# First batch's softmax division at the attention outputs, and the first MoE's weight clamp on GpSimd

## The chip, the cores and the metric

The kernel runs on one core of one Trainium2 chip. The metric is the device time of one execution in microseconds (us). Three runs of the kernel before gave 967.96, 968.99 and 969.51 us, a median of 968.99 us. The engines are TensorE (PE for matmuls, PEld for weight loads), VectorE (DVE), ScalarE (ACT), GpSimd (POOL) and SyncE (SP), which issues the DMAs. Each of them works through its own instructions in order, and waits on semaphores that the others raise.

## The reference, cut to what matters

Three layers follow one another. Attention with a decay comes first (4 batches, 8 heads, 576 positions, 64 wide), then a mixture layer that takes the largest of three products, then a layer with a rational activation.

```python
scores = (q @ k.T) / sqrt(D) + cum[:, None] - cum[None, :]    # causal, cum = cumsum(log(clip(f)))
attn = exp(scores - max(scores))
attn = attn / (sum(attn, axis=-1) + 1e-09)                    # the division of the change
x  = attn @ v                                                 # 2304 tokens x 512
x  = max(x @ w1, x @ w2, x @ w3) @ w_out                      # first MoE, 512 -> 768 -> 512
h  = x @ w_in                                                 # second MoE, 512 -> 2048
g  = (a0 + a1*h + a2*h**2 + a3*h**3) / (1 + |b0|*|h| + |b1|*h**2 + 1e-6)
out = g @ w_out2                                              # 2048 -> 512
```

The weights of both MoE layers arrive in a 64-bit format, read as pairs of 32-bit integers (a low and a top half), and the kernel converts them itself.

## The kernel before, in words

Attention works on pairs of heads. The first batch is cut in two query groups (group 0: the first 320 positions in blocks of 64, 128 and 128; group 1: the last 256 in two blocks), so that it gives eight pairs, numbered 0 to 7: four with group 0, then four with group 1. The other batches give twelve pairs with both groups. A unit is one head of a pair in one group. The main loop takes one unit a step, in three stages that overlap: `scores` of unit s, `turn` of unit s-1, `attend` of the pair when both its heads are turned.

- `scores` (L324) multiplies queries and keys on TensorE. VectorE adds the mask and takes the row maximum (L347, then a read of the accumulator). ScalarE takes the exponential and leaves the row sum in the tile `rs` (L353).
- `normalise` (L355) adds 1e-9 to the row sums (L358) and takes the reciprocal (L359) on VectorE, and GpSimd multiplies every block of exponentials `e` with it in place (L362): three instructions a unit in group 0 (64, 192 and 320 columns), two in group 1 (448 and 576).
- `turn` transposes the blocks on TensorE (L382) into the PSUM tile `tp`, and ScalarE copies them to `pt` (L384).
- `attend` multiplies with v (L398), ScalarE rounds the result to the high part of `x` (L405), and VectorE subtracts to get the low part (L406). Of these two parts every later product is made, in three matmuls.

While the first pairs are worked on, the weights of the first MoE are converted in `convert` (L162), 18 pieces of 128x512 (`cv_w`) and 12 of 128x256 (`cv_wo`): ScalarE takes the absolute value (L169), VectorE clamps it (L170), masks and shifts (L171), and joins the halves in two steps (L172, L175), ScalarE makes the rounded high part (L178), GpSimd the low part (L179). The raw pieces lie in rings of buffers that come free with L175. `fill`, called six times a step, hands out these conversions (0.15 of one a call in the first seven steps, 0.5 later), and from step 9 on the first MoE of the batch that is done: 18 products `h` (L430 to L432), whose maximum is taken on VectorE (L437), then the four output products `x2p` (L455 to L457). In the early pairs (0 to 3), `exercised` adds two matmuls of 512 columns on a tile of identities, `warm`, to every bank that TensorE opens (L84).

The tile framework puts the instructions of each engine into an order that it works out from a model of their durations; the program's order gives the priorities. So a change of one instruction can move many others. Only the second MoE from its seventeenth step on stands in an order written by hand.

## Time and profile before

| | |
|---|---|
| median of three runs | 968.99 us |
| profiled execution | 970.9 us, span 969.1 us |
| mean granted TensorE clock | 0.988 |
| busy: PE, PEld | 943.1 us (97%), 829.9 us (86%) |
| busy: DVE, ACT, POOL | 739.6 us (76%), 623.8 us (64%), 252.4 us (26%) |

The busy time of TensorE counts matmuls that overlap, so it says where the engine stands still more surely than how fast it works. The lines of the change run in the first 160 us, so the rows are read by stage: 11 to 52 us is attention of group 0, 52 to 140 us is attention of group 1 with the first MoE and most of the conversions, 148 to 500 us are the other three batches.

### The profile page before, as it was taken

The page shows a single profiled execution, that of the slowest core. Times are in us where ns is not written, and L with a number is a line of the kernel's source. Part 1 is how long each engine was busy: PE and PEld are TensorE (multiplying, and loading weights), DVE is VectorE, ACT ScalarE, POOL GpSimd, SP SyncE. Part 2 cuts the span into 40 slices and gives each one's busy share as a digit, 9 for nine tenths or more (in the row PEclk, how much of TensorE's full clock was granted, in tenths as well). Part 3 has the DMA queues.
Part 4 walks back from the last instruction along what each step waited for, and adds up shares of the span by engine and source line. Part 5 has one row for each costly group of instructions (what it writes and reads, how often), then busy time and mean ns, then how long its engine had stood idle before and what let it go on. Part 6 is the DMA issues. An engine that isn't in the chain of part 4 may idle for free.

```text
span 969.1 us, 16846 instructions
## 1 busy us (share of the span) xinstructions
PE 943.1 (97%) x5780; PEld 829.9 (86%) x5780; DVE 739.6 (76%) x1756; ACT 623.8 (64%) x1457; POOL 252.4 (26%) x408
## 2 busy tenths in 40 slices
PE   7998999999999999999999999999999999999998
PEld 6767889998998988999999978888888888999997
DVE  5789985557777777534397949988888988899997
ACT  5875666667667666646454548767666766677775
POOL 2646553445454545425133400000000000000000
PEclk9978999999999999999999999999999999999999
DMA  6685233124446445230145477011002101100000
GB/s 160 159 236 153 64 83 89 43 63 119 140 131 205 133 136 174 58 94 1 57 140 185 132 253 269 1 44 43 1 1 66 44 1 46 64 1 1 34 1 33
DMA packets 125621, 88.52 MB, mean 91 GB/s; under 512 B 74448, under 2 KB 110304, under 8 KB 125536
## 3 DMA queue, kind: packets, MB, share of 16 engines
q1 hardware_dynamic: 125536, 87.45, 30.4%
q8 instruction: 46, 0.75, 0.4%
q14 instruction: 39, 0.32, 0.1%
HBM read 64.73 MB, written 22.69 MB: 90 GB/s over the span
## 4 chain that ended last, share of the span: by engine, by line
PE 70%; DVE 14%; DMA 6%; ACT 4%; issue 3%; POOL 2%; SPq 1%; ACTq 0%; POOLq 0%; DVEq 0%
PE oo L721 7%; PE oo L722 7%; PE oo L720 7%; PE hq L671 6%; PE hq L673 6%; PE hq L672 6%; PE tp L382 4%; PE h L430 4%; PE o L398 4%; PE h L431 4%; PE h L432 4%; PE x2p L455 2%; DMA raw_wi<-in_moe_w_in_dram 2%; PE x2p L456 2%; PE x2p L457 2%
## 5 line engine op out<-in xcount | busy, mean ns | idle before, releaser
L430 PE MATMUL h<-x,w1h 128*128 128x320 f32 (+1 forms) x576 | 176.6, 307 | 3.1 <-ACT m L435 2.2
L431 PE MATMUL h<-x,w1h 128*128 128x320 f32 (+1 forms) x576 | 172.1, 299 | 0.0
L432 PE MATMUL h<-x,w1l 128*128 128x320 f32 (+1 forms) x576 | 171.2, 298 | 0.0
L430 PEld LDWEIGHTS h<-x,w1h 128*128 128x128 f32 x576 | 109.4, 190 | 7.0 <-ACT m L435 3.0
L362 POOL TENSOR_SCALAR e<-e,rs 128x64 f32<-128x64 f32 (+4 forms) x160 | 87.7, 563 | 106.4 <-DVE rs L359 91.5
L353 ACT ACTIVATE e<-e,st 128x64 f32<-128x64 f32 (+4 forms) x160 | 89.1, 557 | 37.8 <-DVE st L347 36.0
L721 PE MATMUL oo<-wp,gh 128*128 128x512 f32 x288 | 112.9, 392 | 0.0
L720 PE MATMUL oo<-wp,gh 128*128 128x512 f32 x288 | 112.5, 390 | 0.0
L431 PEld LDWEIGHTS h<-x,w1h 128*128 128x128 f32 x576 | 109.5, 190 | 0.4 <-issue 0.2
L432 PEld LDWEIGHTS h<-x,w1l 128*128 128x128 f32 x576 | 109.2, 190 | 0.0
L722 PE MATMUL oo<-wp,gl 128*128 128x512 f32 x288 | 108.8, 392 | 0.0
L680 ACT ACTIVATE s<-hq 128x512 f32<-128x512 f32 (+1 forms) x80 | 44.3, 554 | 97.4 <-PE hq L673 97.4
L347 DVE CUSTOM_DVE_ANT_0 e<-s,mask 128x320 f32<-128x320 f32 (+3 forms) x160 | 67.2, 433 | 37.9 <-PE s L346 24.0
L384 ACT ACTIVATE pt<-tp 128x384 f32<-128x384 f32 (+3 forms) x160 | 69.8, 469 | 19.2 <-PE tp L382 17.4
L683 DVE SCALAR_TENSOR_TENSOR s<-s,ab,u 128x512 f32<-128x512 f32 (+1 forms) x80 | 55.7, 697 | 32.1 <-ACT u L681 31.9
L382 PE MATMUL tp<-ident,e 128*128 128x128 f32 (+1 forms) x480 | 78.0, 280 | 1.3 <-DVE k2s L275 0.6
L673 PE MATMUL hq<-x,wil 128*128 128x512 f32 (+1 forms) x192 | 70.4, 367 | 0.0
L671 PE MATMUL hq<-x,wih 128*128 128x512 f32 (+1 forms) x192 | 70.4, 367 | 0.0
L672 PE MATMUL hq<-x,wih 128*128 128x512 f32 (+1 forms) x192 | 70.3, 366 | 0.0
L722 PEld LDWEIGHTS oo<-wp,gl 128*128 128x128 f32 x288 | 54.1, 188 | 11.7
L720 PEld LDWEIGHTS oo<-wp,gh 128*128 128x128 f32 x288 | 54.2, 188 | 11.0
L721 PEld LDWEIGHTS oo<-wp,gh 128*128 128x128 f32 x288 | 54.1, 188 | 10.9
(129 smaller groups left out, 2433.6 us busy)
## 6 DMA issues: line engine op xcount, KB each, us to landing
raw_w<-in_moe_w_dram SPq DMA_DIRECT2D x18, 512.0 KB
raw_wp<-in_moe_w_out_dram SPq DMA_DIRECT2D x32, 256.0 KB
wpd<-wp SPq DMA_DIRECT2D x32, 256.0 KB
raw_wi<-in_moe_w_in_dram SPq DMA_DIRECT2D x32, 256.0 KB
wp<-wpd SPq DMA_DIRECT2D x10, 768.0 KB
x2d<-xo SPq DMA_DIRECT2D x16, 320.0 KB
out_dram<-ob SPq DMA_DIRECT2D x18, 256.0 KB
kn<-in_k_dram SPq DMA_DIRECT2D x32, 128.0 KB
```

The source lines that it names most:

```text
L353: nc.scalar.activation(e[:nr], e[:nr], AF.Exp, bias=m, scale=-1.0, accum_out=l)
L362: nc.gpsimd.tensor_scalar(e, e, self.rs[:, 1, j : j + 1], 0.0, op0=ALU.mult, op1=ALU.add)
L382: nc.tensor.transpose(tp[:kr, dst : dst + P], self.e[i][:, Q0[c] : Q1[c]], ident)
L430: nc.tensor.matmul(hp_[:, :w], wh[:, j, dc], xs[dc][:, 1], start=(dc == NDC - 1), stop=False)
L431: nc.tensor.matmul(hp_[:, :w], wh[:, j, dc], xs[dc][:, 0], start=False, stop=False)
L432: nc.tensor.matmul(hp_[:, :w], wl[:, j, dc], xs[dc][:, 0], start=False, stop=(dc == 0))
L671: nc.tensor.matmul(hp_[:, :w], wih[:, dc, fs], xh, start=(dc == 0), stop=False)
L672: nc.tensor.matmul(hp_[:, :w], wih[:, dc, fs], xl, start=False, stop=False)
L673: nc.tensor.matmul(hp_[:, :w], wil[:, dc, fs], xh, start=False, stop=(dc == NDC - 1))
L720: nc.tensor.matmul(o, g[0][:, ts_], wh_, start=(fc == 0), stop=False)
L721: nc.tensor.matmul(o, g[0][:, ts_], wl_, start=False, stop=False)
L722: nc.tensor.matmul(o, g[1][:, ts_], wh_, start=False, stop=(fc == NF2 - 1))
```

## The change: what it does

For the eight pairs of the first batch (`LATE`), `normalise` no longer touches the exponentials. The row sums of the two heads lie in one tile. When the second head is done, VectorE adds 1e-9 and takes the reciprocal for both at once (L369, L370 after), and GpSimd spreads the result over 64 columns a head into a tile `rx` (L374). In `turn`, TensorE transposes `rx`, one matmul a block, into a PSUM tile `rb` from the ring that the other transposes use (L407), and ScalarE copies it to a tile `rn` in SBUF (L411). In `attend`, VectorE multiplies the output with `rn` (L435), ScalarE rounds the product (L436) and VectorE subtracts (L437). Apart from that, the clamp of `convert` goes from VectorE to GpSimd (L171) for the 30 pieces of the first MoE; the pieces named `wp` and `wi`, of the second MoE, keep it on VectorE.

```diff
--- before.py
+++ after.py
@@ -113,6 +113,7 @@
 
 
     LOOK, WHOLE, PRE = 2, 6, 2
+    LATE = NPAIR * 2
     CONV2, EARLY = (32, 0.25), 12
     kqs = {}
 
@@ -167,7 +168,7 @@
         t = pool.tile(shape, I32, name=f"cv_{nm_}", tag=tag, bufs=bufs)
         tf = t.bitcast(F32)
         nc.scalar.activation(tf, top.bitcast(F32), AF.Abs)
-        nc.vector.tensor_scalar(tf, tf, E_LO, E_HI, op0=ALU.max, op1=ALU.min)
+        (nc.gpsimd if nm_[:2] != "wi" and nm_[:2] != "wp" else nc.vector).tensor_scalar(tf, tf, E_LO, E_HI, op0=ALU.max, op1=ALU.min)
         nc.vector.tensor_scalar(t, t, 0x07FFFFFF, 3, op0=ALU.bitwise_and, op1=ALU.logical_shift_left)
         nc.vector.scalar_tensor_tensor(
             out=t, in0=low, scalar=29, in1=t, op0=ALU.logical_shift_right, op1=ALU.bitwise_or
@@ -249,6 +250,7 @@
             self.iq = [[(2 * n + h) % m for h in range(2)] for m in NQB]
             self.pt = {}
             self.whole = n < WHOLE
+            self.late = n < LATE
             self.iqf = [(2 * n + h) % 4 for h in range(2)]
 
         def load(self):
@@ -319,7 +321,13 @@
 
         def begin(self):
             self.st = apool.tile([P, 9], F32, name=f"st_{self.nm}", tag="st", bufs=3)
-            self.rs = apool.tile([P, 2, 3], F32, name=f"rs_{self.nm}", tag="rs", bufs=3)
+            p = self.pair
+            if not p.late:
+                self.rs = apool.tile([P, 2, 3], F32, name=f"rs_{self.nm}", tag="rs", bufs=3)
+                return
+            if self.h == 0:
+                p.rs = apool.tile([P, 2, 2, 3], F32, name=f"rs_{self.nm}", tag="rsd", bufs=2)
+            self.rs = p.rs[:, :, self.h]
 
         def scores(self, i):
             p, h, g = self.pair, self.h, self.g
@@ -355,6 +363,16 @@
         def normalise(self):
             blks = GBLK[self.g]
             n = len(blks)
+            if self.pair.late:
+                if self.h == 1:
+                    rs = self.pair.rs
+                    nc.vector.tensor_scalar_add(rs[:, 0, :, :n], rs[:, 0, :, :n], 1.0e-9)
+                    nc.vector.reciprocal(rs[:, 1, :, :n], rs[:, 0, :, :n])
+                    rx = apool.tile([P, n, 2, D], F32, name=f"rx_{self.nm}", tag=("e3_", "e2_")[self.g] + str(self.pair.hp % 2))
+                    self.pair.rx = rx
+                    r = rs[:, 1, :, :n].rearrange("p h j -> p j h").unsqueeze(3).to_broadcast([P, n, 2, D])
+                    nc.gpsimd.tensor_scalar(rx, r, 1.0, 0.0, op0=ALU.mult, op1=ALU.add)
+                return
             nc.vector.tensor_scalar_add(self.rs[:, 0, :n], self.rs[:, 0, :n], 1.0e-9)
             nc.vector.reciprocal(self.rs[:, 1, :n], self.rs[:, 0, :n])
             for j, i in enumerate(blks):
@@ -382,6 +400,15 @@
                     nc.tensor.transpose(tp[:kr, dst : dst + P], self.e[i][:, Q0[c] : Q1[c]], ident)
                 n += hi - q0
             nc.scalar.activation(pt[:kr, base : base + n], tp[:kr, :n], AF.Copy)
+            if p.late and self.h == 1 and bank == len(GBANK[g]) - 1:
+                lo, w = GQ[g][0], GQ[g][1] - GQ[g][0]
+                rb = ps_t.tile([P, 512], F32, name=f"rb_{self.nm}", tag="t")
+                for j, i in enumerate(GBLK[g]):
+                    nc.tensor.transpose(
+                        rb[:, Q0[i] - lo : Q0[i] - lo + P], p.rx[:, j].rearrange("p h d -> p (h d)"), ident
+                    )
+                p.rb = mpool.tile([P, 320], F32, name=f"rn_{self.nm}", tag="mx", bufs=3)
+                nc.scalar.activation(p.rb[:, :w], rb[:, :w], AF.Copy)
 
         def attend(self):
 
@@ -402,6 +429,13 @@
                         if (j, i) != (0, 1):
                             pinned(mm)
             x = mpool.tile([P, 2, w], F32R, name=f"x_{self.nm}", tag=f"x{g}", bufs=(6, 8)[g])
+            xt[p.b, p.hp, g] = x
+            if p.late:
+                xn = p.rb
+                nc.vector.tensor_tensor(xn[:, :w], ot[:, :w], xn[:, :w], op=ALU.mult)
+                nc.scalar.activation(x[:, 0], xn[:, :w], AF.Copy)
+                nc.vector.tensor_tensor(x[:, 1], xn[:, :w], r32(x[:, 0]), op=ALU.subtract)
+                return
             nc.scalar.activation(x[:, 0], ot[:, :w], AF.Copy)
             nc.vector.tensor_tensor(x[:, 1], ot[:, :w], r32(x[:, 0]), op=ALU.subtract)
             xt[p.b, p.hp, g] = x
```

Three places show what this moves. The first is GpSimd's queue where the pieces of `w_out` are converted (`cv_wo`, then `wo` for the low part; `hh` is the low part of the first MoE's middle layer, `e` an exponential block). This is the kernel before:

```order
L179 TENSOR_TENSOR wo_1065<-cv_wo_0_1066,wo_1065 128x256
L362 TENSOR_SCALAR e_6_1_1_1357<-e_6_1_1_1357,rs_1_1_1356 128x448
L362 TENSOR_SCALAR e_6_1_1_1373<-e_6_1_1_1373,rs_1_1_1356 128x576
L179 TENSOR_TENSOR wo_1065<-cv_wo_1_1117,wo_1065 128x256
L179 TENSOR_TENSOR wo_1165<-cv_wo_0_1166,wo_1165 128x256
L443 TENSOR_TENSOR hh_0_3_1688<-m_0_0_3_1686,hh_0_3_1688 128x320
L179 TENSOR_TENSOR wo_1165<-cv_wo_1_1197,wo_1165 128x256
```

The same pieces in GpSimd's queue after the change:

```order
L171 TENSOR_SCALAR cv_wo_0_1063<-cv_wo_0_1063 128x256
L180 TENSOR_TENSOR w1l_948<-cv_w_5_1016,w1h_947 128x512
L171 TENSOR_SCALAR cv_wo_1_1113<-cv_wo_1_1113 128x256
L180 TENSOR_TENSOR wo_1062<-cv_wo_0_1063,wo_1062 128x256
L171 TENSOR_SCALAR cv_wo_0_1162<-cv_wo_0_1162 128x256
L180 TENSOR_TENSOR wo_1062<-cv_wo_1_1113,wo_1062 128x256
L171 TENSOR_SCALAR cv_wo_1_1193<-cv_wo_1_1193 128x256
L477 TENSOR_TENSOR hh_0_2_1479<-m_0_0_2_1477,hh_0_2_1479 128x320
L180 TENSOR_TENSOR wo_1161<-cv_wo_0_1162,wo_1161 128x256
L180 TENSOR_TENSOR wo_1161<-cv_wo_1_1193,wo_1161 128x256
L171 TENSOR_SCALAR cv_wo_0_1244<-cv_wo_0_1244 128x256
L171 TENSOR_SCALAR cv_wo_1_1264<-cv_wo_1_1264 128x256
```

The two multiplications of `e` are gone from between the subtractions, and each clamp stands behind one or two subtractions of earlier pieces.

The second is VectorE at the same pieces (`m` is a maximum of the first MoE), here in the kernel before:

```order
L170 TENSOR_SCALAR cv_wo_0_1166<-cv_wo_0_1166 128x256
L437 TENSOR_TENSOR m_0_0_3_1615<-m_0_0_3_1546,h_0_0_3_1602 128x320
L171 TENSOR_SCALAR cv_wo_0_1166<-cv_wo_0_1166 128x256
L172 SCALAR_TENSOR_TENSOR cv_wo_0_1166<-raw_wo_0_1063,cv_wo_0_1166 128x256
L175 SCALAR_TENSOR_TENSOR cv_wo_0_1166<-raw_wo_0_1063,cv_wo_0_1166 128x256
L170 TENSOR_SCALAR cv_wo_1_1197<-cv_wo_1_1197 128x256
L171 TENSOR_SCALAR cv_wo_1_1197<-cv_wo_1_1197 128x256
L437 TENSOR_TENSOR m_0_0_3_1686<-m_0_0_3_1615,h_0_0_3_1673 128x320
L172 SCALAR_TENSOR_TENSOR cv_wo_1_1197<-raw_wo_1_1115,cv_wo_1_1197 128x256
L175 SCALAR_TENSOR_TENSOR cv_wo_1_1197<-raw_wo_1_1115,cv_wo_1_1197 128x256
```

VectorE at these pieces after the change:

```order
L172 TENSOR_SCALAR cv_wo_0_1063<-cv_wo_0_1063 128x256
L173 SCALAR_TENSOR_TENSOR cv_wo_0_1063<-raw_wo_0_996,cv_wo_0_1063 128x256
L176 SCALAR_TENSOR_TENSOR cv_wo_0_1063<-raw_wo_0_996,cv_wo_0_1063 128x256
L435 TENSOR_TENSOR rn_1_1_1462<-o_1_1_1517,rn_1_1_1462 128x256
L172 TENSOR_SCALAR cv_wo_1_1113<-cv_wo_1_1113 128x256
L173 SCALAR_TENSOR_TENSOR cv_wo_1_1113<-raw_wo_1_1014,cv_wo_1_1113 128x256
L176 SCALAR_TENSOR_TENSOR cv_wo_1_1113<-raw_wo_1_1014,cv_wo_1_1113 128x256
L437 TENSOR_TENSOR x_1_1_1283<-rn_1_1_1213,x_1_1_1283 128x256
L172 TENSOR_SCALAR cv_wo_0_1162<-cv_wo_0_1162 128x256
L471 TENSOR_TENSOR m_0_0_2_1477<-m_0_0_2_1393,h_0_0_2_1464 128x320
L173 SCALAR_TENSOR_TENSOR cv_wo_0_1162<-raw_wo_0_1060,cv_wo_0_1162 128x256
L176 SCALAR_TENSOR_TENSOR cv_wo_0_1162<-raw_wo_0_1060,cv_wo_0_1162 128x256
```

A piece has three instructions in place of four, the first of which waits for GpSimd's clamp, and the multiplications `rn` and subtractions `x` of the attention outputs stand among them.

The third is TensorE where pair 8, the first of the second batch, begins (`s_0_8_0` and the like are its scores, `h_0_0_4` the fifth of six column blocks of the first MoE, `rb` the transposed reciprocals, `o` an attention output), here in the kernel before:

```order
L455 MATMUL x2p_0_0_2046<-hh_0_5_2004,wo_1488 128x320
L455 MATMUL x2p_0_1_2099<-hh_0_5_2004,wo_1488 128x320
L456 MATMUL x2p_0_0_2046<-hh_0_5_2004,wo_1488 128x320
L457 MATMUL x2p_0_0_2046<-hh_0_5_2004,wo_1488 128x320
L456 MATMUL x2p_0_1_2099<-hh_0_5_2004,wo_1488 128x320
L457 MATMUL x2p_0_1_2099<-hh_0_5_2004,wo_1488 128x320
L345 MATMUL s_0_8_0_0_1694<-k1s_1087,q1s_1621 128x64
L345 MATMUL s_0_8_0_0_1700<-k1s_1087,q1s_1621 128x192
L297 MATMUL tq_1_1633<-ident,qn_1429 128x128 x2
```

TensorE at the first scores of pair 8's second head after the change:

```order
L400 MATMUL tp_7_1_1_1667<-ident,e_7_1_1_1590 64x128
L354 MATMUL s_0_8_1_0_1762<-k2s_1090,q2s_1626 128x64
L353 MATMUL s_0_8_1_0_1768<-k1s_1089,q1s_1625 128x192
L354 MATMUL s_0_8_1_0_1768<-k2s_1090,q2s_1626 128x192
L407 MATMUL rb_1_1_1671<-ident,rx_1_1_1642 128x128 x2
L353 MATMUL s_0_8_1_0_1774<-k1s_1089,q1s_1625 128x320
L354 MATMUL s_0_8_1_0_1774<-k2s_1090,q2s_1626 128x320
L353 MATMUL s_0_8_0_1_1851<-k1s_1084,q1s_1153 128x448
L354 MATMUL s_0_8_0_1_1851<-k2s_1085,q2s_1154 128x448
L425 MATMUL o_1_1_1719<-pt_124,v_1422 64x256 x8
L425 MATMUL o_1_1_1719<-pt_124,v_1422 64x128 x2
L464 MATMUL h_0_0_4_1779<-x_1_0_836,w1h_848 128x320
```

Before, all 18 products `h` and half of `x2p` stand ahead of pair 8's scores. After, the scores stand ahead of the last five products `h` and of all of `x2p`. The transposes of `rx` are new.

## Rows read from the trace of the kernel before

**Rows 1.** Stages: us, busy us of PE, PEld, DVE, ACT, POOL (x instructions), PEclk, DMA share, GB/s.

```profile
11.00:52.00 41.00, 40.05 (x231) 31.25 (x232) 25.02 (x91) 31.59 (x94) 19.02 (x29) 1.00 0.65 171
52.00:62.00 10.00, 9.06 (x50) 5.87 (x48) 9.88 (x27) 8.87 (x23) 2.15 (x4) 1.00 1.13 318
62.00:80.00 18.00, 16.23 (x57) 10.43 (x57) 16.71 (x37) 10.93 (x26) 12.58 (x13) 0.53 0.61 166
80.00:124.00 44.00, 39.38 (x272) 36.19 (x271) 41.21 (x87) 25.92 (x64) 26.69 (x32) 1.00 0.39 112
124.00:140.00 16.00, 14.34 (x104) 12.61 (x102) 14.28 (x45) 12.06 (x33) 8.74 (x12) 1.00 0.18 46
140.00:148.00 8.00, 7.25 (x28) 6.72 (x29) 4.51 (x13) 3.71 (x11) 4.63 (x10) 0.57 0.54 152
148.00:500.00 352.00, 348.13 (x2733) 323.18 (x2732) 218.31 (x738) 221.85 (x637) 154.54 (x276) 1.00 0.37 104
...
570.00:969.00 399.00, 394.71 (x1801) 333.23 (x1799) 349.69 (x569) 275.01 (x490) 0.00 (x0) 1.00 0.14 49
```

**Rows 2.** Chain of waits, 50 to 150 us: start us, us, what.

```profile
58.42 1.47 DVE cv_w L175
...
61.74 0.74 POOL e L362
...
66.30 3.78 PE s L343 x6
```

**Rows 3.** VectorE groups, 52 to 140 us: busy us, mean ns, idle before, releaser.

```profile
L175 DVE SCALAR_TENSOR_TENSOR cv_w<-raw_w,cv_w 128x512 int32<-128x512 int32 x12 | 11.4, 953 | 0.1
...
L175 DVE SCALAR_TENSOR_TENSOR cv_wo<-raw_wo,cv_wo 128x256 int32<-128x256 int32 x12 | 7.0, 586 | 0.2
L170 DVE TENSOR_SCALAR cv_w<-cv_w 128x512 f32<-128x512 f32 x12 | 6.6, 550 | 1.2 <-ACT cv_w L169 1.1
...
L170 DVE TENSOR_SCALAR cv_wo<-cv_wo 128x256 f32<-128x256 f32 x12 | 5.3, 448 | 0.8 <-ACT cv_wo L169 0.8
...
L358 DVE TENSOR_SCALAR rs<-rs 128x2 f32<-128x2 f32 x8 | 3.0, 379 | 0.1
...
L359 DVE RECIPROCAL rs<-rs 128x2 f32<-128x2 f32 x8 | 1.3, 156 | 0.1
L406 DVE TENSOR_TENSOR x<-o,x 128x256 fp32r<-128x256 f32 x3 | 1.2, 416 | 0.5 <-ACT x L405 0.5
```

**Rows 4.** GpSimd busy on L362 alone, 0 to 145 us (x instructions).

```profile
0.00:145.00 145.00, 24.48 (x40) 0.93 0.53 142
```

**Rows 5.** GpSimd groups, 0 to 145 us.

```profile
L179 POOL TENSOR_TENSOR w1l<-cv_w,w1h 128x512 fp32r<-128x512 f32 x18 | 25.3, 1409 | 26.4 <-ACT w1h L178 26.2
L179 POOL TENSOR_TENSOR wo<-cv_wo,wo 128x256 fp32r<-128x256 f32 x12 | 8.8, 741 | 4.1 <-ACT wo L178 4.0
L362 POOL TENSOR_SCALAR e<-e,rs 128x576 f32<-128x576 f32 x8 | 7.2, 898 | 0.0
...
L362 POOL TENSOR_SCALAR e<-e,rs 128x448 f32<-128x448 f32 x8 | 5.7, 709 | 9.2 <-DVE rs L359 9.2
L362 POOL TENSOR_SCALAR e<-e,rs 128x320 f32<-128x320 f32 x8 | 4.7, 586 | 0.0
L362 POOL TENSOR_SCALAR e<-e,rs 128x192 f32<-128x192 f32 x8 | 4.3, 532 | 0.0
```

**Rows 6.** Chain of waits, three TensorE pieces of 10 to 150 us.

```profile
47.82 0.33 PE tp L382 x3
...
143.81 0.27 PE x2p L456
...
148.33 0.14 PE x2p L456
```

**Rows 7.** VectorE line L170, 0 to 160 us: duration ns min/median/max.

```profile
L170 DVE TENSOR_SCALAR cv_w<-cv_w x18: 400/422/1032, 21.6 to 99.7; 128x512 f32<-128x512 f32 x18
```

**Rows 8.** The page's costliest groups: the copy of the transposed weights of attention.

```profile
L384 ACT ACTIVATE pt<-tp 128x384 f32<-128x384 f32 (+3 forms) x160 | 69.8, 469 | 19.2 <-PE tp L382 17.4
```

## Prediction

> **What bounds the kernel now.** I read the table of stages first, then the chain of waits in the stages of the change, then the groups of VectorE and GpSimd there.
>
> The stages fall into three kinds [rows 1]. From 11 to 52 us TensorE is busy 40.05 of 41 us at full clock, much of it with the `warm` matmuls; VectorE is busy 25.0 us of it. From 52 to 140 us VectorE is the fullest: 9.88 + 16.71 + 41.21 + 14.28 = 82.1 of 88 us, or 93%, while TensorE stands still for 10 + 18 + 44 + 16 - (9.06 + 16.23 + 39.38 + 14.34) = 9.0 us, and in 62 to 80 us it has a granted clock of 0.53, the lower of its two levels (1.2 GHz). GpSimd is busy 50.2 of these 88 us. From 148 us on TensorE is busy 348.1 of 352 us, and at the end 394.7 of 399. So time won before 148 us reaches the end unless TensorE itself has to repay it, and nothing in the change shortens what comes behind.
>
> The chain of waits says the same of the middle stage: a join of 1.47 us on VectorE, then a GpSimd multiplication of `e`, then six score matmuls that take 3.78 us at the low clock [rows 2]. VectorE's queue delays the masks, these the exponentials and transposes, and TensorE waits.
>
> **The change part by part.** *What leaves VectorE.* Of the 30 clamps, six of the 18 wide ones lie ahead of 52 us, where VectorE does not bind. The other 12 take 6.6 us and the 12 narrow ones 5.3 us, 11.9 us in all [rows 3]. The 16 instructions on row sums (3.0 + 1.3 = 4.3 us) become eight for two heads each, which saves 2.15 us. Five multiplications by `rn` come in, each priced as the subtraction of `x`, 0.416 us [rows 3], so 2.1 us. Net: 11.9 + 2.15 - 2.1 = 12.0 us less on the engine that binds. The other three pairs' multiplications lie where it does not bind.
>
> *What GpSimd does.* The 40 multiplications of `e` leave: 24.5 us [rows 4]. The clamp on GpSimd is not in the trace. The nearest rows are its own one-input instructions, 898 and 709 ns for 576 and 448 columns, 586 and 532 for 320 and 192 [rows 5]. Between them, 512 columns cost 0.80 us and 256 cost 0.56, so 18 x 0.80 + 12 x 0.56 = 21.1 us. The low end is VectorE's fastest, 0.40 [rows 7], the high end GpSimd's subtraction with two inputs, 1.409 and 0.741 us, so 34.3 us. I take 21.1, as the same engine's same kind of instruction. The eight `rx` tiles (384 or 256 columns) cost 4 x 0.65 + 4 x 0.56 = 4.8 us. So GpSimd has 25.9 us in place of 24.5: even.
>
> *The wait that is added.* VectorE's mask-and-shift now waits for GpSimd, and behind it in VectorE's queue stand masks and maxima that TensorE waits for. The order shows where the clamp stands behind a subtraction of an earlier piece. For narrow pieces the way from the last join of piece n to the clamp of piece n+2 is a ScalarE copy (0.47 us, [rows 8]), a subtraction (0.74) and a clamp (0.56): 1.77 us. Meanwhile VectorE has piece n+1, three instructions of at most 0.586 us [rows 3], 1.76 us. That is a dead heat, decided by what else stands in either queue. The bounds are no wait at all, and one whole subtraction at each of the 24 pieces in the stage, 12 x 1.409 + 12 x 0.741 = 25.8 us. I take a quarter of a microsecond a piece, 6.0 us, near the low end, since GpSimd is idle 43% of the stage and ahead of many wide pieces the clamps stand two together.
>
> *What TensorE gets.* Twenty transposes of `rx` at 0.11 us (three in 0.33, [rows 6]) are 2.2 us, 12 of them in the stage to 52 us, where TensorE binds: 1.3 us. There it also stood idle 0.95 us, part of it for the multiplication of `e`, which no longer lies in the way; I take 0.8 us lost, between 0 and 1.3. In the middle stage the other eight fit into the 9.0 us of idle time. If that cover went, they would cost 0.9 us.
>
> *What ScalarE gets.* Eight copies of `rb`, each at the page's mean for `pt`, 0.469 us [rows 8], are 3.8 us. ScalarE is busy 31.6 of 41 us in the first stage and 57.8 of 88 in the second [rows 1], so idle time hides them; without that cover the four in the first stage would cost 1.9 us.
>
> *What moves.* The last five of 18 products `h` and all of `x2p` now stand behind the first scores of pair 8. This is 60 matmuls of `h` at about 0.14 us (an `x2p` of the same width at full clock, [rows 6]), 8.4 us, which pair 8 gains and which TensorE pays back after it. It changes no sum of work, and I cost it at nothing; but it means that pair 8 may start early by much more than the kernel gains. SyncE's loads keep their sequence nearly unchanged; the raw pieces' buffers come free with the last join, so loads start as much earlier as VectorE gets there. The four to five narrow pieces that stand behind pair 8's masks fall where VectorE has room.
>
> *Sum:* 12.0 - 6.0 - 0.8 = 5.2 us less, of the 9.0 us for which TensorE stands still in the stage. The profiled execution took 970.9 us with a span of 969.1, so the sum makes 965.7 there. It lies 1.9 us above the median of the runs, 968.99, and against that I predict 964.
>
> *A rule that speaks against it.* VectorE's clamps of 512 columns take 400 ns at least and 1032 at most [rows 7], and the joins in the middle stage 953 on average, so VectorE is stretched by something. The Trainium skill says in "SBUF — State Buffer" (SBUF: two separate sides) that GpSimd and VectorE share a pair of ports under an exclusive lock for the whole instruction, for VectorE instructions in a two-port mode or with two SBUF inputs. By that rule every microsecond handed to GpSimd can hold VectorE's joins. The trace agrees that VectorE is stretched, and does not show the lock itself. By the rule the stretch would not change here, since GpSimd's sum stays even; only if the clamps ran at the two-input price, 13 us more, would it grow.
>
> **The rivals.**
>
> *It gains more.* The low clock from 62 to 80 us [rows 1] costs TensorE 0.47 of 16.2 us, 7.6 us, and the one from 140 to 148 us costs 0.43 of 7.25, 3.1 us. Ahead of the first TensorE idled 0.94 of 10 us. If it waits less, it may keep the full clock. With the wait on GpSimd at zero and the first of these gone, 12.0 - 0.8 + 7.6 = 18.8 us is the most, 950. Half of the wait and half of the clock give 12.0 - 3.0 - 0.8 + 3.8 = 12.0 us, 957. For it speaks that the multiplication of `e` stands on the chain just ahead of the slow score matmuls [rows 2]. Against it: VectorE stays at 70 of 88 us and its queue still mixes joins and masks.
>
> *No change.* TensorE is busy 79.0 of 88 us in the middle stage even with its waits. If its overlapped matmuls and the low clock bind it, VectorE's 12 us become idle time there, and the 2.2 us of transposes eat what is won: 0 to 2 us, 968. Against it speaks that from 80 to 124 us the clock is full and VectorE still has 41.2 of 44 us.
>
> *Slower.* The clamps wait in GpSimd's queue. GpSimd's subtraction for w1 already sat idle 26.2 us for ScalarE's high part [rows 5], which itself waits for VectorE. With a clamp behind such a subtraction, VectorE waits for GpSimd, which waits for ScalarE, which waits for VectorE, and the conversion goes in lockstep. It decides from 12.0 - 0.8 = 11.2 us over 24 pieces, 0.47 us a piece. At 0.75 us a piece it costs 18.0 - 11.2 = 6.8 us, 976; at the whole subtraction 25.8 - 11.2 = 14.6 us, 984. For it speaks the order of the narrow pieces; against it that clamps of wide pieces stand ahead of the subtractions.
>
> **How the numbers follow.** The forecast, 960 to 967 in its own range, has 0.40; the larger gain 0.22; no change 0.15; slower 0.23. About 0.2% (1.9 us) is what a measurement of this kernel can tell from no change. Nearly all of the forecast and the larger gain lie beyond it: 0.61 faster, 0.16 the same, 0.23 slower. A range of 954 to 976 leaves out half of the slower case and a third of the larger gain, about 0.19 in all.
>
> **What would show it.** In the profile of the changed kernel VectorE's line for the mask-and-shift (L172 there) shows the idle time ahead of it with GpSimd's clamp (L171) as releaser: about 6 us if I am right, under 2 for the larger gain, over 12 for the slower case. The clamps should take about 0.80 and 0.56 us. VectorE's busy time up to the last narrow join should fall by some 15 us (11.9 for the clamps above, 6 x 0.42 for the other six at the median of [rows 7], 4.3 for the row sums of both stages, less 8 x 0.42 for the multiplications). TensorE's stage with `warm` matmuls should end within 1.3 us of where it did. The first mask of pair 8 should come over 10 us earlier, while steady TensorE work starts only some 5 us earlier. The forecast is wrong if the middle stage does not shorten although VectorE's busy time falls, or if the time is lost behind 148 us, where the order has moved too.

## The result and the profile after

The changed kernel takes 982.86 us at the median (980.48 to 983.08, 4 runs) against 969.25 us (967.96 to 969.55, 4 runs) for the kernel before: a ratio of 1.0137, 95% interval 1.0119 to 1.0156. It is 13.6 us slower, where 5.0 us less were predicted, and outside the range of 954 to 976. The profiled execution took 982.84 us with a span of 981.1.

Line numbers shift in the changed kernel: L170 is ScalarE's magnitude, L171 the clamp, L172 VectorE's mask and shift, L173 and L176 its joins, L179 and L180 the high and low parts, L464 to L466 the products `h`, L471 their maximum.

The same table of stages as in [rows 1], of the kernel after (us, busy us of PE, PEld, DVE, ACT and POOL with instructions, granted clock, DMA share, GB/s; the last one runs to the end):

```profile
11.00:52.00 41.00, 39.00 (x230) 30.49 (x230) 24.57 (x74) 30.89 (x89) 22.31 (x15) 1.00 0.59 160
52.00:62.00 10.00, 9.88 (x55) 6.73 (x54) 7.43 (x22) 8.81 (x23) 7.32 (x5) 1.00 0.93 269
62.00:80.00 18.00, 13.42 (x73) 8.82 (x70) 16.76 (x36) 14.72 (x35) 13.27 (x10) 0.89 0.86 218
80.00:124.00 44.00, 33.23 (x220) 29.77 (x219) 34.30 (x62) 23.72 (x57) 34.63 (x34) 0.85 0.37 101
124.00:140.00 16.00, 11.72 (x63) 9.85 (x63) 13.31 (x35) 10.21 (x29) 10.99 (x13) 0.90 0.29 84
140.00:148.00 8.00, 6.66 (x29) 5.90 (x31) 7.46 (x25) 6.67 (x23) 6.92 (x12) 0.55 0.22 49
...
570.00:990.00 420.00, 406.94 (x1878) 343.98 (x1876) 352.80 (x577) 278.24 (x497) 0.74 (x1) 1.00 0.15 52
```

Until 80 us the balance is even: TensorE is 1.05 us less busy up to 52 us, but has a clock of 0.89 in place of 0.53 from 62 to 80. In 80 to 140 us TensorE is busy 33.23 + 11.72 = 45.0 us, where it was 53.7 [rows 1], and its granted clock is 0.85 and 0.90 where it was 1.00. VectorE, the fullest engine before with 55.5 of these 60 us, is now busy 47.6: it lost work and waits. GpSimd went from 35.4 to 45.6 us.

The groups of GpSimd up to 165 us after, which answer to [rows 5] (busy us, mean ns, idle before, releaser):

```profile
L171 POOL TENSOR_SCALAR cv_w<-cv_w 128x512 f32<-128x512 f32 x18 | 36.3, 2025 | 14.8 <-ACT cv_w L170 14.7
L180 POOL TENSOR_TENSOR w1l<-cv_w,w1h 128x512 fp32r<-128x512 f32 x18 | 24.7, 1378 | 4.9 <-ACT w1h L179 4.8
L171 POOL TENSOR_SCALAR cv_wo<-cv_wo 128x256 f32<-128x256 f32 x12 | 13.1, 1098 | 3.4 <-ACT cv_wo L170 3.1
```

The clamps take 2025 and 1098 ns, not 800 and 560: 49.4 us in place of 21.1. The idle time ahead of the subtraction for `w1l` fell from 26.4 us [rows 5] to 4.9. GpSimd still waits for ScalarE, 14.8 + 3.4 us ahead of the clamps, but now VectorE waits for it in turn.

VectorE's mask and shift, 10 to 170 us after:

```profile
L172 DVE TENSOR_SCALAR cv_w<-cv_w 128x512 int32<-128x512 int32 x18 | 16.1, 895 | 7.0 <-POOL cv_w L171 7.0
...
L172 DVE TENSOR_SCALAR cv_wo<-cv_wo 128x256 int32<-128x256 int32 x12 | 7.6, 637 | 5.3 <-POOL cv_wo L171 5.2
```

It waits 7.0 + 5.2 us for GpSimd's clamp. It also lasts longer (why is read below, from single instructions). These are its two groups (L171 there) of the kernel before in the same stretch, with the clamps (L170) above them:

```profile
L170 DVE TENSOR_SCALAR cv_w<-cv_w 128x512 f32<-128x512 f32 x18 | 9.5, 529 | 3.0 <-ACT cv_w L169 2.8
L171 DVE TENSOR_SCALAR cv_w<-cv_w 128x512 int32<-128x512 int32 x18 | 9.1, 508 | 0.2
...
L170 DVE TENSOR_SCALAR cv_wo<-cv_wo 128x256 f32<-128x256 f32 x12 | 5.3, 448 | 0.8 <-ACT cv_wo L169 0.8
...
L171 DVE TENSOR_SCALAR cv_wo<-cv_wo 128x256 int32<-128x256 int32 x12 | 5.0, 426 | 0.1
```

14.8 us of clamps left VectorE (9.5 + 5.3), and its mask and shift grew from 14.1 to 23.7 us, 9.6 more. Wait and growth are 21.8 us over 30 pieces, 0.73 us a piece, of which the wait is 0.41. One narrow piece in the chain of waits after (start us, us, what) shows how it goes round:

```profile
123.64 0.44 ACT cv_wo L170
124.08 0.08 issue
124.15 1.26 POOL cv_wo L171
125.42 0.02 issue
125.44 0.96 DVE cv_wo L172
126.40 0.02 issue
126.42 0.85 DVE cv_wo L173
127.27 0.02 issue
127.29 0.44 DVE cv_wo L176
127.73 0.02 issue
127.75 0.43 ACT wo L179
128.18 0.07 issue
128.25 0.74 POOL wo L180
128.99 1.04 POOL cv_wo L171
```

ScalarE's magnitude, GpSimd's clamp of 1.26 us, three instructions on VectorE, ScalarE's high part, GpSimd's subtraction, and directly behind it the next clamp: 5.35 us from the start of the first line to that of the last, one engine after the other. What TensorE waited for between 95 and 142 us (engine, line, waited for: us, times, longest):

```profile
PE h L464 <- DVE m L471: 6.6, 2, 5.9
PE tp L400 <- DVE k2s L277: 4.4, 1, 4.4
PE s L353 <- DVE q1s L289: 3.3, 1, 3.3
```

The longest of these ends with a maximum at 123.67 us. Its products had been done at 107 us; it stood in VectorE's queue behind a mask and shift that waited 2.94 us for GpSimd, up to 117.34, and what followed that. That is the queue effect that the prediction named. The two splits, `k2s` at 111.54 and `q1s` at 140.46 us, also come late in VectorE's queue, but directly ahead of them no mask and shift waits for GpSimd.

### The profile page after: what moved, and what is told of

The parts are those of the page before. It is cut to its first block, busy times and chain, and to the rows that moved or that the text cites. A ratio compares the mean times of both kernels' runs of the same rounds, so it can differ in the third digit from the quotient of the medians.

```text
span 981.1 us, 16816 instructions
## 1 busy us (share of the span) xinstructions
PE 944.9 (96%) x5800; PEld 833.7 (85%) x5800; DVE 737.9 (75%) x1718; ACT 630.9 (64%) x1465; POOL 282.0 (29%) x406
## 4 chain that ended last, share of the span: by engine, by line
PE 78%; DVE 11%; issue 3%; POOL 3%; ACT 2%; DMA 2%; SPq 0%; ACTq 0%; DVEq 0%; POOLq 0%
PE hq L705 7%; PE hq L707 7%; PE hq L706 7%; PE oo L755 7%; PE oo L756 7%; PE oo L754 7%; PE h L464 5%; PE h L465 5%; PE h L466 5%; PE o L425 5%; PE tp L400 4%; PE x2p L489 2%; PE s L353 2%; PE s L354 2%; PE x2p L491 2%
## 5 line engine op out<-in xcount | busy, mean ns | idle before, releaser
L464 PE MATMUL h<-x,w1h 128*128 128x320 f32 (+1 forms) x576 | 176.8, 307 | 10.2 <-DVE m L471 6.8
L466 PE MATMUL h<-x,w1l 128*128 128x320 f32 (+1 forms) x576 | 172.4, 300 | 0.0
L464 PEld LDWEIGHTS h<-x,w1h 128*128 128x128 f32 x576 | 110.2, 191 | 13.0 <-DVE m L471 7.7
L755 PE MATMUL oo<-wp,gh 128*128 128x512 f32 x288 | 112.8, 392 | 0.0
L466 PEld LDWEIGHTS h<-x,w1l 128*128 128x128 f32 x576 | 109.9, 191 | 0.0
L380 POOL TENSOR_SCALAR e<-e,rs 128x448 f32<-128x448 f32 (+3 forms) x120 | 64.1, 549 | 79.1 <-DVE rs L377 73.0
L400 PEld LDWEIGHTS tp<-ident,e 128*128 128x128 f32 (+1 forms) x480 | 56.2, 134 | 11.5 <-issue 6.0
L756 PEld LDWEIGHTS oo<-wp,gl 128*128 128x128 f32 x288 | 54.0, 187 | 11.7
L754 PEld LDWEIGHTS oo<-wp,gh 128*128 128x128 f32 x288 | 54.1, 188 | 11.1
```

What stands on the lines that cost most here:

```text
L400: nc.tensor.transpose(tp[:kr, dst : dst + P], self.e[i][:, Q0[c] : Q1[c]], ident)
L464: nc.tensor.matmul(hp_[:, :w], wh[:, j, dc], xs[dc][:, 1], start=(dc == NDC - 1), stop=False)
L466: nc.tensor.matmul(hp_[:, :w], wl[:, j, dc], xs[dc][:, 0], start=False, stop=(dc == 0))
L754: nc.tensor.matmul(o, g[0][:, ts_], wh_, start=(fc == 0), stop=False)
L755: nc.tensor.matmul(o, g[0][:, ts_], wl_, start=False, stop=False)
L756: nc.tensor.matmul(o, g[1][:, ts_], wh_, start=False, stop=(fc == NF2 - 1))
```

## The experiments

Three causes were put against each other: A, the price of the clamp on GpSimd; B, the hand-over from GpSimd to VectorE, whatever the price; C, the work of the division part. D came up after the first four runs: the division part's new tile shares buffers with the maxima of the first MoE, and that moves the products `h`. Each group of runs shared a chip with runs of the kernel before, and ratios are to those (medians of before: 968.48 us for the first four, 967.13 for the next four, 966.89 for the last three).

### Each part alone

The division part alone (the change with this line undone):

```diff
-        (nc.gpsimd if nm_[:2] != "wi" and nm_[:2] != "wp" else nc.vector).tensor_scalar(tf, tf, E_LO, E_HI, op0=ALU.max, op1=ALU.min)
+        nc.vector.tensor_scalar(tf, tf, E_LO, E_HI, op0=ALU.max, op1=ALU.min)
```

> The division part of the change alone: the clamp is back on VectorE for all weights, everything else is as in the changed kernel, and the order of TensorE's work around pair 8 is the changed one (156 of the 216 matmuls of h and none of x2p ahead of pair 8's scores). Theory A (the price of the clamp on GpSimd, 2.0 and 1.1 us for 512 and 256 columns, makes GpSimd's queue the bound): this kernel has no such clamp, so it is not slower than before; the row sums (2.15 us saved) and the five multiplications (2.1 us) cancel on VectorE, 0.8 us of transposes are lost, GpSimd is freed of 24.5 us: 965 to 970 us. Rival C (the division part costs the time: transposes, copies, multiplications, or the products h and x2p that now stand behind pair 8): 977 to 983 us. Rival B (the hand-over from GpSimd to VectorE, whatever the clamp's price): as A here.

Measured: 974.62 us, ratio 1.0061 (1.0047 to 1.0074). It is slower without any clamp on GpSimd, by 6.1 us: A alone falls, B alone too, which expected the same as A here, and C as worded gives too much.

The clamp part alone is the kernel before with only that line changed the other way.

> The clamp part alone: the kernel before, with the clamp of the first MoE's weights on GpSimd; the 40 multiplications of e stay on GpSimd too, and all products h stand ahead of pair 8, as before. Theory A: GpSimd has 49 us of clamps on top of its 50 us of the 88 us between 52 and 140 us (some 36 us of the clamps fall there), so this is slower than before by as much as the changed kernel or more: 983 to 995 us, with clamps of 2.0 and 1.1 us. Rival B: slower as well, 978 to 985. Rival C: about as before or a little faster, 962 to 970.

Measured: 980.20 us, ratio 1.0112 (1.0097 to 1.0128), 11.7 us slower: inside B's range and 3 us below A's. VectorE's mask and shift waits 11.7 us for the wide clamps and 7.8 for the narrow, more than in the changed kernel (7.0 and 5.2). Both parts lose by themselves, and the two losses add up to more than the 13.6 us of the whole change.

### Price or hand-over

In the changed kernel, GpSimd's instruction becomes `tensor_scalar(tf, tf, 1.0, 0.0, op0=ALU.mult, op1=ALU.add)`:

> The changed kernel with GpSimd's clamp replaced by a multiplication by 1.0 and an addition of 0.0: the same engine, tile, place and hand-over to VectorE, but no max and min (the clamp of these weights is left out of the computation). It tells the price of the operation from the wait for another engine. From the multiplications for rx (697 ns for 384 columns, 407 for 256) an estimate is 0.9 and 0.41 us an instruction, 21 us for all 30 in place of 49. Theory A: VectorE's wait at the mask-and-shift falls from 12 us to under 4 and the time to 960 to 968 us. Rival B (the hand-over itself): 978 to 983 us, and the wait stays near 12 us. Rival C: 978 to 983 us too, with the wait gone.

Measured: 975.08 us, 1.0059 (1.0041 to 1.0077). And with `tensor_scalar(tf, tf, E_LO, None, op0=ALU.max)`:

> The changed kernel with max alone in GpSimd's clamp (the min of these weights is left out of the computation). It tells whether the clamp's price lies in the two operations or in the kind of operation. If each of max and min costs its own pass, the instruction takes about half, 1.0 and 0.55 us, 24 us in all, and the time is near the run with multiplication and addition, 960 to 970 us by theory A. If max is slow on GpSimd whether one or two, it stays at 1.6 to 2.0 us and the time at 975 to 983. Rival B: 978 to 983 whatever it takes.

Measured: 980.99 us, 1.0126 (1.0108 to 1.0144), in the range of a slow maximum; the instruction's time lies between the two cases. Line L171 on GpSimd in three kernels (duration ns min/median/max, first and last start): first the changed kernel,

```profile
L171 POOL TENSOR_SCALAR cv_w<-cv_w x18: 1915/1917/2429, 21.7 to 108.8; 128x512 f32<-128x512 f32 x18
L171 POOL TENSOR_SCALAR cv_wo<-cv_wo x12: 1062/1064/1252, 116.2 to 156.4; 128x256 f32<-128x256 f32 x12
```

then with multiplication and addition,

```profile
L171 POOL TENSOR_SCALAR cv_w<-cv_w x18: 607/618/1063, 22.6 to 99.7; 128x512 f32<-128x512 f32 x18
L171 POOL TENSOR_SCALAR cv_wo<-cv_wo x12: 397/405/698, 102.9 to 141.9; 128x256 f32<-128x256 f32 x12
```

then with the maximum alone.

```profile
L171 POOL TENSOR_SCALAR cv_w<-cv_w x18: 1485/1488/1930, 21.6 to 107.3; 128x512 f32<-128x512 f32 x18
L171 POOL TENSOR_SCALAR cv_wo<-cv_wo x12: 839/847/1124, 112.4 to 147.5; 128x256 f32<-128x256 f32 x12
```

The price lies in the kind of operation: 1917 ns with max and min, 1488 with max alone, 618 with multiplication and addition. The cheap operation takes 0.78 points off the ratio, so price does count. But it stays slower by as much as the division part alone, so price is not all, and VectorE's wait only falls from 12.2 to 8.5 us (6.7 + 1.8). A's expectation (960 to 968) failed, and so did that of B and C (978 to 983): price and something else both count.

### Where the division part loses

In the order of instructions, the division part has 156 of 216 matmuls of `h` ahead of pair 8's first scores, where the kernel before has all; the clamp part alone keeps all. The new tile `rn` takes turns with the maxima `m` in the three buffers of `mx`. The next kernel gives `rn` the six buffers of `hh` instead, and all 216 stand ahead again:

```diff
-                p.rb = mpool.tile([P, 320], F32, name=f"rn_{self.nm}", tag="mx", bufs=3)
+                p.rb = mpool.tile([P, 2, 320], F32, name=f"rn_{self.nm}", tag="hh", bufs=6)[:, 0]
```

> The division part alone, as in e1_division, but the tile rn (transposed reciprocals, then quotients) lies in the six buffers of hh in place of the three of mx, which the running maxima m of the first MoE use. With that all 216 matmuls of h stand ahead of pair 8's scores again, as before (156 in e1_division). Theory D (what the division part lost, 6.1 us, it lost by rn taking turns with m in three buffers, which ties the products h to the pace of the attention pairs and moves the last five behind pair 8): 964 to 970 us, and TensorE's busy time from 80 to 148 us at a granted clock of 0.95 or more again until 140 us. Rival C (the part's own work costs it: 20 transposes, eight copies, eight multiplications): 973 to 976 us, as e1_division.

Measured: 965.85 us, 0.9990 (0.9978 to 1.0001). The 6.1 us are gone: the division part's work costs nothing that can be measured, its buffers did. The second way to the same order keeps `rn` in `mx`, with `LATE = 7`:

> The division part alone, as in e1_division, for the first seven pairs in place of eight; rn stays in the buffers of mx. The eighth pair is divided as before. All 216 matmuls of h and 32 of x2p stand ahead of pair 8 in this order, though seven rn still share three buffers with m. If it is the place of the last products h behind pair 8 that costs: 965 to 970 us. If it is the sharing, wherever the products stand: 971 to 975. Rival C: seven eighths of the loss stay, 973 to 974 us.

Measured: 964.54 us, 0.9976 (0.9965 to 0.9987), faster than both kernels, by 0.24% than the one before. The traces tell the pace of the products from their place. The shared buffers do slow the pace: the 11th of the 18 products starts at 118.2 us in the division part alone and at 117.5 with seven pairs, but at 106.4 with `rn` in `hh` and 106.9 before. The slow pace alone costs nothing that can be measured, since seven pairs have it too. What differs is what comes next: with seven pairs the last five products follow from 124 us on, in the division part alone only from 142.9, behind pair 8's first scores at 131.3. So the place of the products decides, and the shared buffers cost by moving them; no run moves the place with nothing else changed. The stages of the division part alone,

```profile
80.00:124.00 44.00, 38.82 (x253) 33.26 (x252) 39.75 (x89) 27.78 (x68) 22.26 (x29) 0.92 0.39 102
124.00:140.00 16.00, 12.04 (x60) 8.78 (x60) 15.22 (x54) 13.73 (x44) 7.90 (x16) 0.75 0.24 60
140.00:148.00 8.00, 8.00 (x53) 6.77 (x50) 4.39 (x14) 3.19 (x9) 4.13 (x8) 0.85 0.18 41
```

with `rn` in the buffers of `hh`,

```profile
62.00:80.00 18.00, 14.85 (x71) 9.33 (x72) 17.04 (x40) 14.56 (x35) 5.65 (x5) 0.81 0.90 248
80.00:124.00 44.00, 41.99 (x297) 37.88 (x296) 41.41 (x96) 27.44 (x72) 22.86 (x29) 1.00 0.34 93
124.00:140.00 16.00, 12.63 (x73) 10.69 (x74) 15.30 (x49) 12.79 (x38) 8.06 (x14) 0.79 0.30 72
140.00:148.00 8.00, 8.00 (x61) 7.45 (x58) 5.23 (x18) 5.68 (x18) 6.55 (x12) 1.00 0.18 41
```

and with seven pairs:

```profile
80.00:124.00 44.00, 38.74 (x251) 33.16 (x251) 40.08 (x91) 28.00 (x70) 22.93 (x29) 0.92 0.38 103
124.00:140.00 16.00, 16.00 (x116) 15.97 (x115) 15.22 (x44) 10.88 (x30) 11.47 (x16) 1.00 0.11 25
140.00:148.00 8.00, 7.90 (x60) 6.65 (x60) 5.45 (x23) 5.81 (x20) 4.77 (x12) 1.00 0.42 124
```

Busy time by granted clock in 80 to 148 us is TensorE's work in us at full clock (an estimate, since both are means of a stage): 38.82 x 0.92 + 12.04 x 0.75 + 8.00 x 0.85 = 51.5 for the division part alone, 60.0 and 59.5 for the two others, 57.8 before [rows 1, with 140 to 148 us], and 42.5 after. Against the kernel before that is 6.3 less, 2.2 and 1.7 more, and 15.4 less, and the medians moved by +6.1, -1.3, -2.6 and +13.6 us. By these stages alone the version with four pairs (below) has 5.2 more and is no faster, so the stretch is cut too short. From 62 us on, and against the times of the profiled executions themselves (970.9 us before), the estimate of TensorE's work follows the time of all twelve other kernels here to within 2 us, such as 12.1 less and 11.9 us slower for the whole change, 3.1 less and 4.4 slower for the division part alone, 4.5 more and 2.6 faster for four pairs. TensorE makes up later what it did not do here, at full clock: it is busy 406.94 us from 570 us on after (the last line of the first table), and 394.71 before [rows 1].

> The division part alone for the first four pairs, which all lie ahead of the first MoE, so that no rn is there at the same time as a maximum m; the pairs 4 to 7 are divided as before. It tells the part's cost in the stage to 52 us, where TensorE is full, from its cost in the middle stage. Theory D: 965 to 970 us (12 transposes at 0.11 us, 1.3 us, against GpSimd's multiplications out of the way). Rival C: half of the loss or more, 971 to 975 us.

Its edit is `LATE = NPAIR`. Measured: 968.43 us, 1.0015 (1.0006 to 1.0024). That is 1.3 us, as much as 12 transposes were estimated to take in the stage to 52 us, and the last `warm` matmul starts 1.7 us later than before (56.8 us); that the transposes are the cause is not shown.

### Price and hand-over again, with the order kept

The whole change with `rn` in the buffers of `hh`:

> The whole change, with rn in the buffers of hh as in e5_division_hh: the clamp is on GpSimd, and all h stand ahead of pair 8. Theory A with D: the loss to the order goes, the loss to the clamp's price stays: as much slower than e5_division_hh as the changed kernel is slower than e1_division, 8 us, so 972 to 979 us. If the two losses are one (the clamp only costs because of the order), 964 to 970; if rn's place doesn't matter with the clamp on GpSimd, 981 to 984.

Measured: 973.25 us, 1.0066 (1.0052 to 1.0080). The clamps cost 7.4 us here (against `rn` in `hh` alone) as they do with `rn` in `mx` (982.86 against the division part alone, by ratios), so this loss does not hang on the order. Then the same with multiplication and addition on GpSimd, and with no instruction there:

> As e8_both_hh, with GpSimd's clamp replaced by a multiplication by 1.0 and an addition of 0.0 (the clamp of these weights is left out of the computation): 0.62 and 0.40 us an instruction (medians of e3_multadd) in place of 1.92 and 1.06. With the products h ahead of pair 8 this is the prediction's own case, a clamp at GpSimd's one-input price. Theory A with D: 957 to 963 us, faster than e5_division_hh by 3 to 9 us (12 us off VectorE less a wait). Rival B (the hand-over eats what VectorE gains, whatever the price): 964 to 968, as e5_division_hh.

> As e9_multadd_hh, with no instruction at all in the clamp's place (the clamp of these weights is left out of the computation): VectorE loses the 11.9 us of clamps of the middle stage and waits for ScalarE alone. It bounds what taking the clamps off VectorE can be worth. If VectorE is what bounds the middle stage: 952 to 958 us, 8 to 12 us below e5_division_hh. If TensorE's clock or another engine takes over: 959 to 965. The difference from e9_multadd_hh is the price of the hand-over.

Measured: 964.45 us, 0.9974 (0.9963 to 0.9985), just above A's range with D and inside B's (964 to 968): at the low price the hand-over eats most of what VectorE gains. And 958.54 us, 0.9914 (0.9898 to 0.9930), 7.3 below the one with `rn` in `hh` and between its two cases. What the narrow mask and shift waited for in the first of these, 10 to 170 us,

```profile
DVE cv_wo L172 <- POOL cv_wo L171: 1.5, 3, 0.6
```

and in the second:

```profile
DVE cv_wo L172 <- ACT cv_wo L170: 1.9, 4, 1.0
```

The difference of 5.9 us is the hand-over at a low price. The waits show 1.2 of it (with those of the wide pieces, at the end of the next two lines, 5.1 against 3.9). The wide mask and shift also lasts longer, which could be most of the rest. Its group behind the cheap instruction:

```profile
L172 DVE TENSOR_SCALAR cv_w<-cv_w 128x512 int32<-128x512 int32 x18 | 13.3, 750 | 3.8 <-POOL cv_w L171 3.6
```

The same group with no instruction there:

```profile
L172 DVE TENSOR_SCALAR cv_w<-cv_w 128x512 int32<-128x512 int32 x18 | 9.0, 502 | 2.3 <-ACT cv_w L170 2.0
```

18 instructions at 750 ns behind GpSimd and 502 ns behind ScalarE: 4.3 us. That these reach the end in full is not shown.

Why the mask and shift lasts longer shows in its single instructions. In all 13 kernels, a wide one with no GpSimd instruction running beside it takes 430 ns at most; the longer ones, up to 1782 ns, all have one beside them. With no instruction in the clamp's place 12 of the 18 run alone, behind the cheap one 6, in the changed kernel 5. Behind a clamp the mask and shift starts just as GpSimd starts on its next instruction. One such place of the changed kernel (start us, us, instruction):

```profile
94.07 1.92 POOL L171 TENSOR_SCALAR cv_w<-cv_w 128x512 f32<-128x512 f32 x1
95.95 1.28 POOL L180 TENSOR_TENSOR w1l<-cv_w,w1h 128x512 fp32r<-128x512 f32 x1
96.02 1.49 DVE L172 TENSOR_SCALAR cv_w<-cv_w 128x512 int32<-128x512 int32 x1 [0.88 <-POOL cv_w L171]
```

When the clamp has ended, at 95.99 us, GpSimd's subtraction has just started and the mask and shift starts. It ends at 97.51 us, 0.28 us behind the subtraction. Five more of the 18 wide ones end 0.28 to 0.29 us behind a subtraction that started just ahead of them. Not every GpSimd instruction has this effect: two that start beside a clamp long under way take 414 and 398 ns.

Last, both remedies together, with the clamp on VectorE:

> The version that the runs so far point to: division at the outputs for seven pairs, as e6_seven, rn in the buffers of hh, as e5_division_hh, the clamp on VectorE. If the two remedies are one and the same (h ahead of pair 8), it lies at 963 to 967 us, no better than either; if the shared buffers cost something beside the order, 959 to 963.

Measured: 965.39 us, 0.9983 (0.9969 to 0.9997): they are one remedy. Of the versions that compute everything, seven pairs is the lowest at 0.9976, with an interval that overlaps those of the other two.

## Why the prediction was wrong

The ratios stand in a row in which each kernel differs from the one ahead of it by one step, and a step is taken as the difference of ratios times 968 us. With the intervals of the ratios a step is known to about 2 us, and it depends on what it is added to: with `rn` in `mx`, max and min cost 7.6 us in place of 8.9.

| step | ratio | us | the prediction's term |
|---|---|---|---|
| division part, `h` ahead of pair 8 | 0.9990 | -1.0 | +0.75 (transposes 0.8, row sums -2.15, multiplications 2.1) |
| clamps gone from VectorE | 0.9914 | -7.4 | -11.9 |
| a cheap instruction on GpSimd in their place | 0.9974 | +5.8 | +6.0 |
| max and min in place of the cheap one | 1.0066 | +8.9 | 0 |
| `rn` in `mx`, five `h` behind pair 8 | 1.0137 | +6.9 | 0 |

Two steps failed. The first is "I take 21.1, as the same engine's same kind of instruction". GpSimd's multiplications were taken as the price of its maxima. They are as cheap as said or cheaper (618 and 405 ns at the median), but max and min take 1917 and 1064 ns, above the bound of 1.409 and 0.741 us as well. With 49.4 us in place of 21.1, and 4.4 for `rx`, GpSimd has 53.8 us in place of 24.5: its sum is not even.

The second is "It changes no sum of work, and I cost it at nothing". The order had been seen and the 8.4 us of `h` counted, but they were taken as payable later. They had been what fills TensorE while pair 8's splits and masks pass through VectorE: with them ahead of pair 8 it is busy 16.00 us from 124 to 140 us (seven pairs), with the last five behind it 12.04. (With `rn` in `hh` it is 12.63 us, but there it had done them by then: 41.99 us busy from 80 to 124 us in place of 38.82.) In the division part alone the clock is then 0.75 from 124 to 140 us and 0.85 up to 148, where seven pairs have 1.00, and what TensorE pays back displaces other work at full clock. That `rn` shares three buffers with `m` stood in the diff (`tag="mx", bufs=3`) and was not used.

The other terms stand better, but not all for their reasons. The step of a cheap instruction is 5.8 us, where 6.0 were put down as a wait. That is luck: the waits show 1.2 of it, and for the stretched mask and shift, which can be most of the rest, the prediction had no term. The prediction's own case, a cheap instruction with `h` ahead of pair 8, measures 0.9974, 2.5 us less, half of the 5.0. The clamps on VectorE are worth 7.4 us, not 11.9: without them the granted clock is 1.00 at every stage,

```profile
62.00:80.00 18.00, 15.34 (x101) 11.86 (x100) 16.94 (x39) 15.68 (x39) 7.92 (x7) 1.00 1.07 291
80.00:124.00 44.00, 41.71 (x294) 37.45 (x293) 41.17 (x99) 31.02 (x82) 24.32 (x31) 1.00 0.33 87
124.00:140.00 16.00, 13.33 (x95) 10.85 (x93) 12.44 (x42) 12.74 (x39) 10.79 (x22) 1.00 0.28 63
140.00:148.00 8.00, 8.00 (x63) 7.25 (x62) 5.34 (x16) 5.67 (x15) 5.32 (x12) 1.00 0.30 79
```

and TensorE is busy 41.71 of 44 us from 80 to 124 us, so little is left for VectorE to give there: with the clamps on VectorE and `rn` in `hh` it was busy 41.99. By busy time and clock, TensorE does 3.3 us more from 62 to 80 us and 3.4 from 124 to 140, where the clock had been 0.81 and 0.79. So this gain comes in the two stages of a low clock, as the rival of a larger gain had it for the first. In the changed kernel that clock also rose, from 0.53 [rows 1] to 0.89, and the time was lost behind it.

The slower rival, with 0.23, had the mechanism of the clamp: lockstep of the conversion, with 0.47 us a piece as the point from which it decides and 976 us at 0.75 a piece. The profile shows 0.73 a piece, but only 0.41 of that is the wait that it meant; the rest is the stretched mask and shift. With the order kept the whole change takes 973.25 us. What brings it to 982.86 is the order, which no rival had, so that the time lies between this rival's 976 and 984 is luck.

Of the signs, the wait ahead of the mask and shift came out at 12.2 us, the slower case's "over 12". The first mask of pair 8 is at 141.95 us in the trace, 1.3 us earlier than before (143.21), not over 10. The last `warm` matmul starts at 57.3 us, 2.2 us later than before (55.1), not within 1.3. VectorE's busy time up to the last narrow join did not fall by 15 us: it is 117.9 us up to 159.4 us, and was 112.8 up to 138.6, since the last pieces now stand behind pair 8's masks and the mask and shift takes longer. The last sign, a middle stage that does not shorten although VectorE's busy time falls, did come: VectorE is busy 47.6 us from 80 to 140 us in place of 55.5, and pair 8 begins no earlier than those 1.3 us.

The rule of the Trainium skill that spoke against the change ("SBUF — State Buffer", SBUF: two separate sides) would have GpSimd's work stretch the joins, which have two inputs in SBUF. The trace agrees with it, instruction by instruction, better than the prediction said: in the changed kernel the six wide joins with no GpSimd instruction beside them took 681 to 694 ns, the 30 others 679 to 1751. Their sum hardly grew, from 42.7 to 44.1 us for the four groups of joins from 10 to 170 us, although GpSimd is busy 66.2 us from 52 to 140 us (sum of the first table) in place of 50.2. What grew is the mask and shift, which has one input, and which behind a clamp starts together with GpSimd's next instruction; whether it runs in the two-port mode that the rule also names, no run here shows.

Another page of the Trainium skill bears on the failed step: "GPSIMD Engine Reference", 4.1 Engine selection, lists add, mul and max together and calls one-input work on GpSimd roughly line-rate. For multiplication with addition the trace comes nearer to that (618 ns for 512 columns, VectorE's clamp 426) than for max and min (1917), where it does not agree.

## What to carry to other kernels

The price of an operation on another engine is not that of its neighbour of the same form: max and min need a row of their own, and where there is none the range should reach beyond the nearest rows. A short-lived tile put into a buffer set that a running chain uses ties that chain's pace to the tile's; compare the order of the engine that must stay full, and cost work that moves behind a bottleneck as filler lost, not as work deferred. A hand-over per piece to another engine cost 5.8 us for 30 pieces here, most of what it was meant to save, and only the smaller part of that is seen as a wait: look at how long the instruction behind the hand-over takes, and at what runs beside it.

## What the runs showed of the hardware

GpSimd's duration on 128 partitions goes with the operation: from the medians at 256 and 512 columns, 3.33 ns a column for max and min ((1917 - 1064) / 256), 2.50 for max alone, 0.83 for multiplication and addition, each with about 0.2 us beside it. VectorE's clamp has 0.55 ((426 - 286) / 256, medians of the division part alone).

A VectorE mask and shift of 128x512 took 430 ns at most in every kernel here when no GpSimd instruction ran beside it, and up to 1782 ns when one did; behind a GpSimd subtraction that started just ahead of it, it ended 0.28 to 0.29 us after that subtraction (six times in the changed kernel).
